# Seven products instead of eight for the second matrix of the block pairs too, with feature-major sums turned in 32x32 blocks and stored so

## The chip, the cores and the metric

The kernel runs on one core of one Trainium2 chip. The metric is the device time of one execution in microseconds (us); lower is better. The time before is the median of three runs, 1665.45 us (1663.57 to 1666.79).

## The reference

```python
# attention without softmax, per batch and head, then an RMS norm over the head's features
kv  = einsum('bhsd,bhse->bhde', k, v);  out = einsum('bhsd,bhde->bhse', q, kv)
x   = out / sqrt(mean(out*out, -1) + 1e-6) * g_norm      # as 4608 tokens x 512 features
# first layer:  w_in 512x2048, w_out 2048x512
x   = (s * max(x @ w_in1, 0)**2 + b) @ w_out1
# second layer, the same sizes
h   = x @ w_in2
out = (h * sigmoid(h)) @ w_out2                            # 4608 x 512, float32
```

## The kernel before, in words

The 4608 tokens are nine blocks of 512. Every factor of a product is split into a rounded part (hi) and a remainder (lo), and a product of 128x128 by 128x512 is three TensorE matmuls: hi by hi, hi by lo, lo by hi. Weights are decoded, split and, for the second layer, spilled to DRAM during the first layer (`decode`, `factors`, L234 to L356).

The first layer works block by block: a `unit` (16 per block) makes 128 hidden features (`mm1`, 12 matmuls) and adds their part to four output tiles (`mm2`, 12 matmuls).

In the second layer, blocks 0 to 7 go as four pairs, `tp` 0 to 3, and block 8 goes last, by units again. `pair_x` loads a pair and forms four differences of its quarters. `hidden(tp, j)`, for j 0 to 7 (`NS` = 8), makes 256 hidden features for the two blocks by Strassen's seven products instead of eight: 7 products x 2 halves x 3 = 42 matmuls at L839, into three PSUM banks X, Y, Z. VectorE adds the banks up at L864 (five instructions of a j), ScalarE copies one (L195), applies SiLU (L883, L885) and rounds the four results (`hi`, L188), and GpSimd or VectorE subtracts for the remainders (`lo`, L191).

`outputs(tp, j)` multiplies by the second matrix in the ordinary way, 8 token tiles (2 blocks x 4) x 2 halves f x 3 = 48 matmuls a j at L933, L934 and L935. The hidden tile is the stationary factor, and the weight tile moves, so a result is a tile of 128 tokens x 512 features in one of four PSUM banks `acc`. For j = 0 it is copied into one of eight tiles `y2`; for the others VectorE adds it to that tile (L943). After j = 7 each tile is stored by one DMA whose rows are 2 KB long (`store`).

All of it is ordered by `Plan`. Each piece of work is added with the engines that it may run on, a cost, a key (its due time), facts that it needs and makes, and the buffers that it takes and gives. `Plan.run` plays these costs through and emits the instructions in the order that results, each on one engine's in-order queue. All large DMAs are issued from SyncE's queue (SP) through the helper `dma` (L200). A wait therefore also holds all that is behind it on the same engine. Buffers: weight tiles of the first layer come free in its last block and are lent to the second layer (`wanted`, `lent_to`): 14 for the pair's split inputs `xo`, 6 for `win` (tiles of the first matrix), 5 for `wout` (of the second), 7 for `g2` (hi and lo of a hidden tile).

Of the kernel before, what the change touches and what calls it, by code (L numbers as in the profile page):

```python
# [15 lines left out]
class Plan:  # L16
# [12 lines left out]
    def __init__(self, room):  # L29
        self.room, self.ops, self.users, self.place = room, [], {}, {}  # L30
# [10 lines left out]
    def run(self):  # L41
# [6 lines left out]
        slots = {}  # L48
# [14 lines left out]
        def begin(e, op, when):  # L63
            t = max(free[e], when)
            for tag, _ in op[6]:
                s = slots.get(tag)
                if s is None:
                    room = self.room.get(tag, 1)
                    s = slots[tag] = [(0.0, i) for i in (range(room) if isinstance(room, int) else room)]
                if not s:  # L70
                    return None
                t = max(t, min(s)[0])
# [3 lines left out]
        while done < len(self.ops):  # L76
# [28 lines left out]
            for b in op[7]:  # L105
                users[b] -= 1
                known[b] = max(known.get(b, 0.0), end)
                if not users[b]:
                    slots.setdefault(b[0], []).append((known[b], self.place[b]))
# [10 lines left out]
def kernel(  # L120
# [40 lines left out]

    EXP_SCALE = 2.0 ** -112
# [36 lines left out]
    def dma(dst, src):  # L199
# [6 lines left out]
    plan = Plan({"g": 2, "acc": 4, "h": 2, "at": 2, "kv": 1, "rem": 1, "q": 1, "part": 2, "rms": 2, "gh": 3, "y": 2,  # L206
                 "raw": 4, "dw": 4, "raw2": 2, "dw2": 1, "tmp": 8})
# [367 lines left out]

    def place(b):

        tag = plan.place[b]
        return (pools["late"] if tag in [f"w{kd}{m}" for kd, m in late] else wp).tile([P, 2, DM], F32R, tag=tag, name=b[0])
# [17 lines left out]
    def unit(u):  # L597
# [7 lines left out]
        def w_gives(kind):  # L605
            if layer:
                return [("win" if kind == "i" else "wout", ("last", m))]
            return [(lent_to[f"w{kind}{m}"], f"w{kind}{m}")] if t == NB - 1 else []
# [9 lines left out]
        for kk in range(KD):  # L618
# [3 lines left out]
                gives=[xs_of(lb, kk)] * (m == KF - 1) + w_gives("i"))  # L622


        g = ("g", u)
        gs = ("gh", u)

        def first(e):
            g_t[u] = tp.tile([P, T], F32, tag="g", name="g", bufs=2)
# [13 lines left out]
        def pair():  # L643
            return (tp.tile([P, T], F32R, tag="gh", name="gh", bufs=3), tp.tile([P, T], F32R, tag="gl", name="gl", bufs=3))

# [11 lines left out]
        def g_hi(e):  # L657
            st["g"] = pair()
# [32 lines left out]
        for d in range(KD):  # L691
            acc = ("acc", (lb, d))
            add({"PE": 0.648}, u + LAG2 + d * 0.02, mm2(d),
                needs=[("gh", u), ("gl", u)] + ready("o") + [("mm2o", u - 1, d)] * (m > 0) + [("mm2o", u, d - 1)] * (d > 0),
# [15 lines left out]
    def block_out(layer, t, d, key, acc):  # L710
        lb = layer * NB + t
        st = {}
        yb = ("y", (lb, d))

        final = lb == 2 * NB - 1

        def out_y(e):
            if not final:
                st["y"] = tp.tile([P, T], F32, tag="y", name="y", bufs=2)
# [42 lines left out]
    def pair_x(tp, kk, key):  # L762
# [17 lines left out]
        def sub(o, a, b_, needs, takes=()):  # L780
# [4 lines left out]
            add(both(T), key + 1 + 0.1 * o, go, needs=needs, makes=[("pxs", o) + me], takes=takes)  # L785
# [308 lines left out]
```

## Time and profile before

| | |
|---|---|
| median of three runs | 1665.45 us |
| profiled execution, from first to last instruction (span) | 1664.5 us |
| TensorE busy | 98% of the span, 7762 matmuls |
| VectorE / ScalarE / GpSimd busy | 51% / 40% / 34% |
| DMA | 236.3 MB, 142 GB/s on average |
| granted TensorE clock | 0.999 of the full 2.4 GHz |

The profile shows one execution of the program. For each engine it gives the time in which the engine was busy; matmuls overlap one another in it, so the duration of one matmul (some 390 ns) is longer than the distance from one start to the next. Beside each wait it names what ended it. The profiled execution has no other time of its own than the span; it is 0.95 us less than the median of the runs.

In the trace, the first layer lasts to about 900 us, the pairs of the second layer from 902 us to about 1570 us (some units of block 8 are mixed in from 1559 us), and the units of block 8 from there to the end.

### The profile page before, as it was taken

How to read it: one execution, taken by the hardware profiler on the slowest of the kernel's cores; microseconds unless marked ns; L12 is line 12 of the kernel's file. 1: busy time of each engine (PE TensorE's matmuls, PEld its weight loads, DVE VectorE, ACT ScalarE, POOL GpSimd, SP SyncE). 2: the span in 40 equal slices, each digit the busy share in tenths (PEclk: the TensorE clock that was granted, in tenths of full speed). 3: DMA queues.
4: the chain of work that ended last, by engine and by line, in shares of the span. 5: the costliest groups of instructions: out<-in, count | busy, mean ns of one | idle time of the engine just before them, and what ended most of it. 6: DMA issues, size and time to landing. Idle time of an engine off the chain costs nothing.

```text
span 1664.5 us, 21283 instructions
## 1 busy us (share of the span) xinstructions
PE 1638.8 (98%) x7762; PEld 1331.6 (80%) x7762; DVE 846.4 (51%) x1301; ACT 664.5 (40%) x1205; POOL 569.6 (34%) x486
## 2 busy tenths in 40 slices
PE   8889999999999999999999999999999999999998
PEld 6667878888888888888887888888878888888887
DVE  5997555566655665534343244534453445244311
ACT  5776444444444444433333422432244224422322
POOL 3774343334434344210231222532253225222200
PEclk9999999999999999999999999999999999999999
DMA  9654335444444544310124444654455446544563
GB/s 217 175 161 137 124 122 158 126 163 134 138 139 129 168 119 155 104 68 0 51 79 145 124 142 141 198 181 140 141 191 181 140 141 203 179 141 140 184 190 108
DMA packets 227032, 236.30 MB, mean 142 GB/s; under 512 B 99952, under 2 KB 181872, under 8 KB 226800
## 3 DMA queue, kind: packets, MB, share of 16 engines
q1 hardware_dynamic: 226800, 234.94, 45.7%
q8 instruction: 62, 1.02, 0.3%
q14 instruction: 42, 0.34, 0.1%
q0 software_dynamic: 128, 0.00, 0.0%
HBM read 181.41 MB, written 53.48 MB: 141 GB/s over the span
## 4 chain that ended last, share of the span: by engine, by line
PE 90%; DVE 5%; issue 2%; DMA 1%; SPq 1%; ACT 1%; POOL 0%; DVEq 0%; POOLq 0%; ACTq 0%
PE hp L839 18%; PE h L184 8%; PE h L185 8%; PE h L183 8%; PE acc L183 8%; PE acc L184 7%; PE acc L185 7%; PE acc L934 7%; PE acc L935 7%; PE acc L933 7%; PE kv_ps L433 1%; DVE raw L263 1%; PE acc L686 1%; PE acc L687 1%; PE acc L688 1%
## 5 line engine op out<-in xcount | busy, mean ns | idle before, releaser
L839 PE MATMUL hp<-xo,win 128*128 128x512 f32 x1344 | 344.6, 391 | 1.8 <-DVE tmp L864 1.2
L191 POOL TENSOR_TENSOR g<-tmp,g 128x512 fp32r<-128x512 f32 x123 | 159.1, 1294 | 423.0 <-ACT g L188 215.5
L839 PEld LDWEIGHTS hp<-xo,win 128*128 128x128 f32 x1344 | 251.9, 188 | 59.4 <-DVE tmp L864 3.0
L943 DVE TENSOR_TENSOR y<-acc,y 128x512 f32<-128x512 f32 x224 | 154.2, 690 | 274.9 <-PE acc L935 272.7
L630 ACT ACTIVATE g<-h 128x512 f32<-128x512 f32 x160 | 95.3, 596 | 352.4 <-PE h L185 352.4
L183 PE MATMUL acc<-gh,wo 128*128 128x512 f32 x576 | 232.6, 404 | 0.0
L184 PE MATMUL acc<-gl,wo 128*128 128x512 f32 x576 | 225.7, 392 | 4.3 <-POOL gl L191 3.3
L185 PE MATMUL h<-xh,wi 128*128 128x512 f32 x576 | 225.6, 392 | 3.4 <-DVE wi L191 3.4
L184 PE MATMUL h<-xl,wi 128*128 128x512 f32 x576 | 226.0, 392 | 1.5 <-POOL xl L191 0.8
L183 PE MATMUL h<-xh,wi 128*128 128x512 f32 x576 | 226.4, 393 | 0.3 <-ACT g L630 0.3
L185 PE MATMUL acc<-gh,wo 128*128 128x512 f32 x576 | 225.4, 391 | 0.6 <-DVE wo L191 0.6
L935 PE MATMUL acc<-wout,g 128*128 128x512 f32 x512 | 201.7, 394 | 0.0
L934 PE MATMUL acc<-wout,g 128*128 128x512 f32 x512 | 201.6, 394 | 0.0
L638 DVE SCALAR_TENSOR_TENSOR g<-g,vecs 128x512 f32<-128x512 f32 x128 | 102.5, 801 | 194.3 <-ACT g L630 194.1
L933 PE MATMUL acc<-wout,g 128*128 128x512 f32 x512 | 201.2, 393 | 0.0
L864 DVE TENSOR_TENSOR tmp<-hp,tmp 128x512 f32<-128x512 f32 x160 | 110.3, 690 | 98.6 <-PE hp L839 93.2
L191 POOL TENSOR_TENSOR spill<-dw,spill 128x512 fp32r<-128x512 f32 x57 | 76.2, 1337 | 177.0 <-ACT spill L188 166.8
L666 DVE SCALAR_TENSOR_TENSOR gl<-g,vecs,gh 128x512 fp32r<-128x512 f32 x128 | 110.4, 863 | 47.3 <-ACT gh L660 46.3
L282 POOL TENSOR_TENSOR dw<-raw 128x256 uint32<-128x256 uint32 (+1 forms) x100 | 87.2, 872 | 137.8 <-DVE raw L268 70.4
L185 PEld LDWEIGHTS h<-xh,wi 128*128 128x128 f32 x576 | 108.5, 188 | 28.0 <-DVE wi L191 5.0
L184 PEld LDWEIGHTS h<-xl,wi 128*128 128x128 f32 x576 | 108.6, 188 | 25.8 <-POOL xl L191 1.4
L184 PEld LDWEIGHTS acc<-gl,wo 128*128 128x128 f32 x576 | 108.4, 188 | 25.4 <-POOL gl L191 4.2
(120 smaller groups left out, 2296.6 us busy)
## 6 DMA issues: line engine op xcount, KB each, us to landing
win<-wi SPq DMA_DIRECT2D x96, 512.0 KB, 4.3
wout<-wo SPq DMA_DIRECT2D x160, 256.0 KB, 4.2
wi<-spill SPq DMA_DIRECT2D x32, 512.0 KB, 2.6
wo<-spill SPq DMA_DIRECT2D x32, 512.0 KB, 2.7
win<-wi SPq DMA_DIRECT2D x64, 256.0 KB, 3.0
raw<-in_moe_w_out_dram SPq DMA_DIRECT2D x38, 256.0 KB, 3.2
y<-y SPq DMA_DIRECT2D x36, 256.0 KB, 2.8
raw<-in_moe_w_in_dram SPq DMA_DIRECT2D x34, 256.0 KB, 2.9
```

The source lines that it names most:

```text
L183: nc.tensor.matmul(ps, wh, xh, start=first, stop=False)
L184: nc.tensor.matmul(ps, wh, xl, start=False, stop=False)
L185: nc.tensor.matmul(ps, wl, xh, start=False, stop=last)
L191: eng[e].tensor_tensor(lo, src, f32(hi), op=ALU.subtract)
L638: nc.vector.scalar_tensor_tensor(out=g_t[u], in0=g_t[u], scalar=s_t, in1=g_t[u], op0=ALU.mult, op1=ALU.mult)
L666: nc.vector.scalar_tensor_tensor(out=st["g"][1], in0=g_t[u], scalar=b_t, in1=f32(st["g"][0]), op0=ALU.add, op1=ALU.subtract)
L839: nc.tensor.matmul(ps, w[:, wn, f_], x_[:, xn], start=first and n == 0, stop=kk == KH - 1 and n == 2, skip_group_check=True)
L864: nc.vector.tensor_tensor(t, bank[me, a], tmp[b_, me], op=ALU.add)
L933: nc.tensor.matmul(ps, g[:, 0, dd], w[:, 0], start=f == 0, stop=False)
L934: nc.tensor.matmul(ps, g[:, 0, dd], w[:, 1], start=False, stop=False)
L935: nc.tensor.matmul(ps, g[:, 1, dd], w[:, 0], start=False, stop=f == 1)
L943: nc.vector.tensor_tensor(y2[tp, tt], st["ps"], y2[tp, tt], op=ALU.add)
```

## The change

`outputs` is done by seven products as well. For each pair there are now four groups `q` of two `j` each, and for each q the seven products (`ORDER`) by two feature tiles (`KH` = 2): 14 steps of 2 x 3 matmuls, where two j had 16 steps of six. The weight tile is now the stationary factor, and a hidden tile moves, so the sums `y2` are 128 features x 512 tokens, fourteen of them for a pair (tiles `ya`). For this `hidden` forms, from its four SiLU results, four differences (`minus`) and splits seven tiles instead of four; the second matrix is loaded with all seven combinations (7 tiles of 512 KB for two j, was 4). At the end of a pair, `results` combines the 14 sums by 14 additions on GpSimd into eight tiles, VectorE turns each in 32x32 blocks (`turn_y`), and four DMAs store each tile in pieces of 32 features, 128 bytes.

The buffers change with it: `win` 5, `wout` 4, `g2` 8 lent tiles and two new ones, and the first layer's `gh` tiles join them (`heir`), thirteen in all; the 14 `ya` tiles are the first layer's `xh` and `xl` (eight), two `g`, two `y` and one lent weight tile in halves. `both2` gives the planner higher costs for two-input instructions.

```diff
+    def both2(n):
+        return {DVE: 0.15 + n * 2.05e-3, POOL: 0.15 + n * 2.25e-3}
...
@@ hidden
-        for f, n, src, ready, kk in ((0, 0, "d", ...), (1, 1, "b", ...), (1, 0, "c", ...), (0, 1, "a", ...)):
...
+        add(both2(T), kt, minus("e", "a", "d"), needs=sg("a", "d"), makes=sg("e"), takes=[tb["e"]])
+        add(both2(T), kt + 0.02, minus("f", "b", "e"), needs=sg("b", "e"), makes=sg("f"), takes=[tb["f"]])
+        add(both2(T), kt + 0.01, minus("a", "b", "a"), needs=sg("b", "e"), makes=sg("a2"))
+        add(both2(T), kt + 0.1, minus("c", "c", "f"), needs=sg("f") + [("gl",) + me + (B21,)], makes=sg("c2"))
+        for i, src, ready, kk, gives in (
+            (B11, "d", sg("d"), k(3) + 0.1, []), (B22, "b", sg("b"), k(4) + 0.2, []), (B21, "c", sg("c"), k(5) + 0.2, []),
+            (T1, "e", sg("e"), kt + 0.03, []), (T3, "a", sg("a2"), kt + 0.05, ["a"]), (T2, "f", sg("f"), kt + 0.07, []),
+            (T4, "c", sg("c2"), kt + 0.12, ["c"]),
+        ):
...
+            add(act(T), kk, hi, needs=ready, makes=[("gh",) + me + (i,)], takes=[gb])
+            add(both2(T), kk + 0.03, lo, needs=[("gh",) + me + (i,)], makes=[("gl",) + me + (i,)],
...
+    ORDER = (B11, B22, B21, T1, T3, T2, T4)
+    NG = NS // 2
...
@@ wout_loads: one tile for a product i of two j
+                for a in range(2):
+                    dma(f32(t)[:, a], w2_d["o", 2 * q + a][:, i])
...
@@ outputs
-                    for f in range(2):
-                        g, w = g2[me, f, n], wo_t[tp, j, f]
-                        nc.tensor.matmul(ps, g[:, 0, dd], w[:, 0], start=f == 0, stop=False)
-                        nc.tensor.matmul(ps, g[:, 0, dd], w[:, 1], start=False, stop=False)
-                        nc.tensor.matmul(ps, g[:, 1, dd], w[:, 0], start=False, stop=f == 1)
+        steps = [(i, d) for i in ORDER for d in range(KH)]
+        for n, (i, d) in enumerate(steps):
...
+                for a in range(2):
+                    (gh, gl), w = g2[(tp, 2 * q + a), i], wo_t[tp, q, i][:, a]
+                    nc.tensor.matmul(ps, w[:, 0, dd], gh, start=a == 0, stop=False)
+                    nc.tensor.matmul(ps, w[:, 0, dd], gl, start=False, stop=False)
+                    nc.tensor.matmul(ps, w[:, 1, dd], gh, start=False, stop=a == 1)
...
+                if q == 0:
+                    y2[tp, i, d] = sums(ya)
+                    copy(e, y2[tp, i, d], st["ps"])
+                else:
+                    nc.vector.tensor_tensor(y2[tp, i, d], st["ps"], y2[tp, i, d], op=ALU.add)
...
+    def results(tp):
+        key = base(tp) + 4 * NS + 8 + LAG3
+        for d in range(KH):
...
+            for n, (i, j, needs, gives) in enumerate((
+                (T2, B11, [t(T2), t(B11)], []), (B21, B11, [t(B21), t(B11)], [B11]), (T3, T2, [t(T3), o(0)], []),
+                (B22, T1, [t(B22), t(T1)], []), (B22, T2, [o(3), o(0), o(2)], [T2]), (T1, T3, [o(2), o(3)], []),
+                (T4, T3, [t(T4), o(2), o(5)], [T3]),
+            )):
...
+                add({POOL: 1.3}, key + 0.02 * n, go, needs=needs + ([o(0)] if n == 1 else []), makes=[o(n)], gives=[y(x) for x in gives])
+            for c, n, i, ready in ((0, 0, B21, 1), (0, 1, B22, 4), (1, 1, T1, 5), (1, 0, T4, 6)):
...
+                def turn_y(e, st=st, z=z, i=i, d=d):
+                    st["z"] = sums(z)
+                    nc.vector.transpose(st["z"], y2[tp, i, d])
...
+                    for a in range(P // Q):
+                        dma(out[r:r + T, f_ + a * Q:f_ + (a + 1) * Q].rearrange("(b r) d -> r b d", r=Q),
+                            st["z"][a * Q:(a + 1) * Q].rearrange("p (b d) -> p b d", d=Q))
+                add(dve(T), key + 0.2, turn_y, needs=[o(ready)], makes=[("yz", tp, c, n, d)], takes=[z], gives=[y(i)])
+                add({"SP": 1.92}, key + 0.3, store, needs=[("yz", tp, c, n, d)], makes=[("out", tp, c, n, d)], gives=[z], move=1.2)
...
@@ unit: block 8's second matrix starts only behind the last step of the pairs
+                + [("omo", NPR - 1, NS // 2 - 1, 13)] * (layer == 1 and m == 0),
...
-        wanted = [f"xo{i}{kk}" for i in range(7) for kk in range(KH)] + ["win"] * 6 + ["wout"] * 5 + ["g2"] * 7
+        wanted = [f"xo{i}{kk}" for i in range(7) for kk in range(KH)] + ["win"] * 5 + ["wout"] * 4 + ["g2"] * 8 + ["ya"]
```

How the change moves the work shows at three places. In the rows, a line's number is that of the kernel it stands in, the tile written is left of the arrow, and a wait stands in brackets (a name such as DMAHW3 is a DMA's semaphore). In the program of before, `y` is also the name of the tiles that hold `y2`.

TensorE, in the middle of the first pair: a step of `outputs` between products of `hidden` (`hp`), before.

```order
L933 MATMUL acc<-wout,g_8620 128x512
L934 MATMUL acc<-wout,g_8620 128x512
L935 MATMUL acc<-wout,g_8620 128x512
L839 MATMUL hp<-xo_7731,win 128x512 [waits DMAHW3_49,DVE_49]
L839 MATMUL hp<-xo_7731,win 128x512 x2
L839 MATMUL hp<-xo_7940,win 128x512 x3
L933 MATMUL acc<-wout,g_8566 128x512
```

The same place now.

```order
L993 MATMUL acc<-g_8559,wout 128x512 [waits DMAHW6_49]
L994 MATMUL acc<-g_8559,wout 128x512
L995 MATMUL acc<-g_8559,wout 128x512
L993 MATMUL acc<-g_8729,wout 128x512 [waits DMAHW7_49]
L994 MATMUL acc<-g_8729,wout 128x512 [waits Pool_49]
L995 MATMUL acc<-g_8729,wout 128x512
L875 MATMUL hp<-xo_7960,win 128x512 x3
```

A step is six matmuls as before, and its two halves now take the hidden tiles of two j as the moving factor. The pairs' steps are 224 now and were 256, and all that TensorE does ahead of the pairs is the same.

SyncE's queue, where the first pair's results are stored, before.

```order
L200 DMA wout<-wo_1_92 128x2x256 [waits DMAHW1_49]
L200 DMA out_dram<-y_8374 128x512 [waits DMAHW2_49,DVE_49]
L200 DMA out_dram<-y_8380 128x512 [waits DMAHW3_49,DVE_49]
L200 DMA out_dram<-y_8395 128x512 [waits DMAHW4_49,DVE_49]
L200 DMA out_dram<-y_8417 128x512 [waits DMAHW5_49,DVE_49]
L200 DMA out_dram<-y_8435 128x512 [waits DMAHW6_49,DVE_49]
L200 DMA x_9524<-y_81 128x2x512 [waits DVE_49,DMAHW7_49,Activation_49,Pool_49]
```

The same place now.

```order
L199 DMA win<-wi_2_85 128x1024 [waits DMAHW6_49,PE_49]
L199 DMA out_dram<-ya 32x16x32 [waits DMAHW7_49,DVE_49]
L199 DMA out_dram<-ya 32x16x32 [waits DMAHW0_49]
L199 DMA out_dram<-ya 32x16x32 [waits DMAHW1_49]
L199 DMA out_dram<-ya 32x16x32 [waits DMAHW2_49]
L199 DMA wout<-wo_0_91 128x512 [waits DMAHW3_49,PE_49]
L199 DMA wout<-wo_1_92 128x512 [waits DMAHW4_49]
L199 DMA win<-wi_2_85 128x512 [waits DMAHW5_49,PE_49]
```

Eight stores of a pair have become 32, each of 512 pieces, and they stand between loads of weights; they come behind the loads of the next pair's inputs, where five of eight stood ahead of the second of these.

ScalarE, where the next pair's first sums are copied out of PSUM, before.

```order
L195 COPY y_9655<-acc 128x512 [waits DMAHW2_49,PE_49]
L195 COPY y_9664<-acc 128x512 [waits DMAHW3_49,PE_49]
L195 COPY y_9669<-acc 128x512 [waits DMAHW4_49,PE_49]
L883 ACTIVATE tmp<-hp 128x512 [waits PE_49]
L188 ACTIVATE g_9685<-tmp 128x512 [waits Activation_49]
L195 COPY y_9691<-acc 128x512 [waits DMAHW5_49,PE_49]
```

The same place now.

```order
L194 COPY ya<-acc 128x512 [waits PE_49]
L919 ACTIVATE tmp<-hp 128x512 [waits PE_49]
L187 ACTIVATE g_9924<-tmp 128x512 [waits Pool_49]
L187 ACTIVATE g_9926<-tmp 128x512 [waits Activation_49]
L194 COPY ya<-acc 128x512 [waits DMAHW2_49,DMAHW6_49,DMAHW1_49,DMAHW7_49,DMAHW0_49,PE_49]
L194 COPY ya<-acc 128x512 [waits DVE_49,PE_49] x2
L921 ACTIVATE tmp<-tmp 128x512 [waits DVE_49]
```

A copy that took a tile waited for one store to land; now six of the fourteen copies wait for the four stores of a tile, and the others for the additions on GpSimd or the turns on VectorE. Behind them on ScalarE are the readings of the banks `hp` that TensorE fills next.

## Rows read from the trace of the kernel before

**Rows 1.** The profile page: span and busy time of each engine.

```profile
span 1664.5 us, 21283 instructions
PE 1638.8 (98%) x7762; PEld 1331.6 (80%) x7762; DVE 846.4 (51%) x1301; ACT 664.5 (40%) x1205; POOL 569.6 (34%) x486
```

**Rows 2.** Waits of TensorE from 900 to 1560 us: total, times, longest.

```profile
PE hp L839 <- DVE tmp L864: 1.2, 2, 0.8
PE hp L839 <- POOL xo L191: 0.6, 1, 0.6
```

**Rows 3.** Windows: length, busy of PE, PEld, DVE, ACT, POOL, clock, DMA share, GB/s.

```profile
920.00:1060.00 140.00, 140.00 (x612) 114.43 (x611) 55.87 (x81) 45.16 (x74) 41.64 (x33) 1.00 0.43 134
1060.00:1100.00 40.00, 40.00 (x174) 32.21 (x173) 21.59 (x29) 18.07 (x30) 21.35 (x16) 1.00 0.72 246
1100.00:1220.00 120.00, 120.00 (x524) 97.94 (x523) 49.27 (x72) 36.48 (x60) 35.35 (x28) 1.00 0.47 145
1390.00:1430.00 40.00, 40.00 (x176) 32.68 (x175) 19.95 (x28) 17.66 (x30) 18.81 (x14) 1.00 0.74 250
```

**Rows 4.** Timeline of TensorE in the first pair's stretch, start and duration in us.

```profile
1121.30 0.40 PE L933 MATMUL acc<-wout,g 128*128 128x512 f32 x1
...
1122.69 1.52 PE L839 MATMUL hp<-xo,win 128*128 128x512 f32 x6
1124.06 0.40 PE L933 MATMUL acc<-wout,g 128*128 128x512 f32 x1
```

**Rows 5.** Timeline, TensorE, two steps of the second pair's stretch, spaced more closely.

```profile
1222.04 0.39 PE L933 MATMUL acc<-wout,g 128*128 128x512 f32 x1
...
1223.39 1.52 PE L839 MATMUL hp<-xo,win 128*128 128x512 f32 x6
```

**Rows 6.** Groups by form, POOL and DVE, 920 to 1550 us: busy us, mean ns.

```profile
L191 POOL TENSOR_TENSOR g<-tmp,g 128x512 fp32r<-128x512 f32 x116 | 150.0, 1294 | 380.7 <-PE acc L935 194.9 <-ACT g L188 173.3 <-PE hp L839 6.2
L784 POOL TENSOR_TENSOR xt<-x,xt 128x512 f32<-128x512 f32 x10 | 15.7, 1566 | 4.5 <-DMA x<-y 4.0
L943 DVE TENSOR_TENSOR y<-acc,y 128x512 f32<-128x512 f32 x211 | 145.2, 690 | 263.4 <-PE acc L935 261.2 <-DMA win<-wi 2.1
L191 DVE TENSOR_TENSOR g<-tmp,g 128x512 fp32r<-128x512 f32 x5 | 7.7, 1530 | 3.6 <-ACT g L188 3.6
```

**Rows 7.** Groups by form, all of the span.

```profile
L191 DVE TENSOR_TENSOR gl<-g,gh 128x512 fp32r<-128x512 f32 x16 | 11.1, 692 | 74.4 <-ACT gh L188 74.4
L536 DVE STREAM_TRANSPOSE sq<-rms 128x512 f32<-128x512 f32 x36 | 25.5, 707 | 0.9
L885 ACT ACTIVATE tmp<-tmp 128x512 f32<-128x512 f32 x96 | 60.6, 632 | 158.2 <-DVE tmp L864 158.1
```

**Rows 8.** The profile page, DMA issues: count, KB each, median us to landing.

```profile
wout<-wo SPq DMA_DIRECT2D x160, 256.0 KB, 4.2
out_dram<-y SPq DMA_DIRECT2D x32, 256.0 KB, 6.0
q<-in_q_dram SPq DMA_DIRECT2D x112, 72.0 KB, 2.9
```

**Rows 9.** DMA view, 240 to 250 us: packets, and the queue's share of 16 engines.

```profile
DMA packets 253, 0.97 MB, mean 97 GB/s; under 512 B 16, under 2 KB 16, under 8 KB 253
q1 hardware_dynamic: 253, 0.97, 24.6%
```

**Rows 10.** The same view, 360 to 370 us.

```profile
DMA packets 3443, 1.82 MB, mean 182 GB/s; under 512 B 2706, under 2 KB 3218, under 8 KB 3442
q1 hardware_dynamic: 3442, 1.80, 61.3%
```

**Rows 11.** Issues on SP's queue, by tile: ns min/median/max, first and last start.

```profile
L200 SPq DMA_DIRECT2D lent_wo<-in_q_dram x16: 465/500/1507, 3.2 to 17.5; - x16
L200 SPq DMA_DIRECT2D out_dram<-y x32: 332/356/713, 1065.7 to 1658.8; - x32
L200 SPq DMA_DIRECT2D out_dram<-x x8: 472/569/597, 1650.4 to 1661.2; - x8
```

**Rows 12.** Timeline of the end: TensorE's last matmul, and SP's last issues.

```profile
1659.01 0.39 PE L688 MATMUL acc<-wout,gl 128*128 128x512 f32 x1
1659.37 2.40 SPq L200 DMA_DIRECT2D out_dram<-x  x4
```

More of the change, by code (lines that the diff above doesn't have):

```diff
@@ L47, in run @@
         ready = {e: {} for e in engines}
-        slots = {}
+        slots = {tag: [(0.0, i) for i in (range(n) if isinstance(n, int) else n)] for tag, n in self.room.items()}
         users = dict(self.users)
@@ L65, in begin @@
             for tag, _ in op[6]:
[L66 to L69, printed above, removed]
+                s = slots.setdefault(tag, [(0.0, 0)])
                 if not s:
@@ L160 @@
     NPR = (NB - 1) // 2
+    NTMP = 9
     EXP_SCALE = 2.0 ** -112
@@ L621, in unit @@
                 makes=[("mm1", u, kk)], opens=[("mm1o", u, kk)], takes=[("h", u)] * (kk == 0),
-                gives=[xs_of(lb, kk)] * (m == KF - 1) + w_gives("i"))
-        g = ("g", u)
-        gs = ("gh", u)
+                gives=([xs_of(lb, kk)] if lb != NB - 1 else [("ya", f"xh{kk}"), ("ya", f"xl{kk}")]) * (m == KF - 1) + w_gives("i"))
+        g = ("tmp" if layer else "g", u)
+        gs = ("g2" if layer else "gh", u)
+        if layer == 0 and u >= NB * KF - 3:
+            plan.heir[gs] = "g2"
+            if u >= NB * KF - 2:
+                plan.heir[g] = "ya"
         def first(e):
-            g_t[u] = tp.tile([P, T], F32, tag="g", name="g", bufs=2)
+            if layer:
+                g_t[u] = pools["l2p"].tile([P, T], F32, tag=f"tmp{plan.place[g]}", name="g")
+            else:
+                g_t[u] = tp.tile([P, T], F32, tag=plan.place[g], name="g")
             nc.scalar.activation(g_t[u], h_t[u], AF.Relu if layer == 0 else AF.Silu)
@@ new lines, in hidden, with minus, go @@
+            add(act(T), kk, silu, needs=ready, makes=[("sg", src) + me], takes=[tb["d"]] if src == "d" else [],
+                gives=[bk[X]] if src == "d" else [])
+        def minus(o, a, b_):
+            def go(e):
+                t = tmp[o, me] if (o, me) in tmp else new(o)
+                eng[e].tensor_tensor(t, tmp[a, me], tmp[b_, me], op=ALU.subtract)
+            return go
+        sg = lambda *names: [("sg", x) + me for x in names]
+        kt = k(6) + 0.2
+        add(both2(T), kt, minus("e", "a", "d"), needs=sg("a", "d"), makes=sg("e"), takes=[tb["e"]])
@@ L1054 @@
                 win_loads(pr, j)
+                hidden(pr, j)
+            for j in range(NG):
                 wout_loads(pr, j)
-                hidden(pr, j)
                 outputs(pr, j)
+            results(pr)
         load_x(2 * NB - 1, KF * (2 * NB - 2) + 2)
@@ L1062 @@
             unit(u)
+        for kk in range(KD):
+            for x in "hl":
+                plan.settle(("ya", f"x{x}{kk}"), f"x{x}{kk}")
         plan.run()
```

158 lines of the change are left out of this document (90 added, 68 removed).

## The prediction

> **What bounds the kernel now.** I read the page's busy times first, then TensorE's waits in the stretch that the change touches, then that stretch by windows, and last single rows for the prices. The page shows TensorE busy for 98% of 1664.5 us [rows 1]. The reader is to see next that between 900 and 1560 us it waited three times, 1.8 us in all [rows 2], and that VectorE, ScalarE and GpSimd are busy for some 30 to 55% of the windows there [rows 3]. So the pairs' stretch is bound by the number of matmuls, and work taken from TensorE there shortens the kernel until something else comes late. The cause for that would stand at the end of a pair, where DMA is already busy for 72 and 74% of a 40 us window, against 43 to 47% between [rows 3].
>
> **The price of a matmul.** The windows from 920 to 1060 and from 1100 to 1220 us hold 612 and 524 matmuls in 260 us with no gap [rows 3]: 0.229 us each. Six of `outputs` take 1.39 us from start to start, the six of `hidden` behind them 1.37 us [rows 4]; 0.231 is the price of a removed one. In some steps six take 1.35 us, 0.225 each [rows 5], so the rate depends on something that these rows don't name; I keep 0.225 and 0.234 (the two sides of the common 0.231) as bounds for the new form, whose stationary factor is the weight tile. The duration of a matmul is 0.39 us [rows 4], and by that the sum would be 75 us instead of 44. The Trainium skill, Perfetto Trace Analysis, Identifying the Most-Contended Engine, warns that matmul busy time tells little of the headroom, since matmuls are pipelined; the rows agree, as starts stand 0.23 us apart.
>
> **What is removed.** A pair had 8 j x 48 matmuls of `outputs`; now it has 4 q x 84. That is 48 less per pair and 192 in all, 1344 for 1536. 192 x 0.231 = **44.4 us** off the path. With all 1344 at 0.225 it would be 8 us more, at 0.234 4 us less. The 1344 matmuls of `hidden` and all of the first layer stay as they are.
>
> **What is added beside TensorE.** A pair lasts 672 x 0.229 = 154 us now, where it lasted 165.
>
> - GpSimd: by the order it gets some 82 two-input instructions a pair, of which 14 are the additions of `results`. At 1294 ns, the usual price, that is 106 us; at 1566 ns, the dearest row, 128 [rows 6].
> - VectorE: some 43 two-input instructions on SBUF, between 692 ns [rows 7] and 1530 ns [rows 6]; 82 evictions of PSUM at 690 ns [rows 6], fewer than before, since `outputs` has 14 for 16; and 8 turns, for which I take the 707 ns of the transposes of the same size [rows 7]. Together 92 to 128 us.
> - ScalarE: three more roundings a j at about the 632 ns of its other SBUF passes [rows 7], 15 us a pair on an engine that was busy for about a third.
>
> None of these reaches 154 us, so on average TensorE covers them. If that cover went, GpSimd would be the first to show, at 128 of 154.
>
> - Loads: the second matrix is 14.7 MB a pair instead of 8.4. The view from 240 to 250 us, with nearly no small packets, gives 24.6% of 10 us for 0.97 MB, 2.54 us of all sixteen engines for 1 MB [rows 9]. The added 6.3 MB take 16 us, spread over the pair.
> - Stores: a tile is 2048 pieces of 128 bytes. From 360 to 370 us, 61.3% of 10 us less 1.80 MB x 2.54 leaves 1.56 us for 2706 small packets, 0.58 us for a thousand [rows 10]. A tile then takes 0.67 + 1.19 = 1.85 us, the eight of a pair 14.8 us, where 2 KB rows took 5.3. These small packets are reads; for writes this is an estimate from them.
>
> In sum a pair has 25 us more of DMA: 49% of 165 us was 81 (43% of 140 and 72% of 40 us [rows 3]), now 107 of 154. In the 40 us at a pair's end it is 29 [rows 3] + 9.5 + 4 = 43 us: full, by little.
>
> - SP's queue: 32 issues of stores at a pair's end for eight. A similar load of 18 x 32 pieces takes 465 to 1507 ns to issue, median 500 [rows 11]; so 15 to 48 us. By the order the eight turns lie within 1.4 j of `hidden`, some 95 matmuls or 22 us. At the median the issues fit.
> - What is queued behind: loads of `win` and `wout` stand between the stores. A pair uses 32 `win` tiles, one in 4.8 us; with five tiles, four may be ahead, 19 us, less the landing, 4.2 us for the like loads [rows 8]: loads may come 15 us late before TensorE stands.
>
> **The waits at a pair's end** are the unknown. The 14 `ya` tiles hold a pair's sums until GpSimd has added, VectorE has turned and the stores have landed. On ScalarE six copies of the next pair's first sums wait for stores, on VectorE turns wait for GpSimd; the readings of `hidden`'s banks stand behind both, and TensorE waits for those. Before, copies also waited for a store's landing, 6.0 us at the median [rows 8], and the longest wait of TensorE was 0.8 us [rows 2]. So the lower bound is nothing; the upper, by 48 us of issues in 22, is 26 late less 15 of cover, 11 us a boundary. I take 2.5 us, near the lower bound, since median issues and transfers just fit, at three boundaries (the fourth lies beside block 8): **+7.5 us**.
>
> **Start and end.** In the first two j there are no steps of `outputs` between, and remainders lag: **+1 us** (the row before shows 0.8 [rows 2]). At the end, steps of `outputs` no longer stand between the last units, and the last four tiles of block 8 come together. SP then has eight issues of 0.57 us [rows 11] behind the first, where four took 2.40 us after the last matmul [rows 12]: 2.3 us more, of which 1.3 are won by the first tile's being done earlier. **+1 us.** A unit's SiLU, rounding and remainder, 0.6 + 0.6 + 0.7 us [rows 7], are covered by 12 matmuls, 2.7 us, so nothing more.
>
> **The sum:** 1664.5 - 44.4 + 7.5 + 1 + 1 = 1629.6, against the profiled execution's 1664.5 us, which has no time but its span and lies 0.95 us below the median of the runs: **1630 us**.
>
> **Rivals.**
>
> 1. *Clean boundaries and closely spaced steps.* If the stores hide as those of before did, and the new form runs at 0.225, the time is 1664.5 - 44.4 - 8 + 2 = 1614 us. For it: the waits of before. Against: most steps ran at 0.23.
> 2. *Short writes cost more than short reads.* At twice the price eight tiles take 29.6 us of DMA, the 40 us window holds 58, and loads come 18 us late, 3 more than the cover: 9 us at three boundaries, 1639. At two and a half times it is 25 late and 10 uncovered, 1661. I put this case at 1650. No row has many such writes. The Trainium skill, DMA: Bandwidth & Descriptors, Specifications, gives 512 bytes as the least for full rate and has smaller transfers done as read-modify-write; no run here shows it yet. By that rule the doubling, 1639 us, is the nearer end.
> 3. *The stores' landings become a chain* (the side of slower). If each tile's landing lets the next one go, a tile takes 4 issues of 0.5 us and a landing of 6.0 [rows 8, 11], 8 us, and eight take 64 where the order gives 22. Of the 42 us, four PSUM banks cover about 11 (four steps of 2.7 us with `hidden` between); 31 us are lost at three boundaries, 93 in all: 1664.5 - 44.4 + 2 + 93 = 1715 us. It decides from 14 us a boundary on. For it: six of fourteen copies wait for four landings each. Against: two to four tiles can be on their way at once, and the eight landings that were waited for cost nothing before.
>
> That the change doesn't remove the matmuls can be left out, as the order shows them gone.
>
> **How the numbers follow.** My forecast, 1620 to 1640, has 0.58; the first rival 0.16, the second 0.15, the third 0.11. What a measurement here can tell from no change is about 0.2%, 3.3 us: faster is below 1662. A fifth of the second rival, 0.03, falls within that of no change; so faster 0.86, same 0.03, slower 0.11. The range reaches from the first rival's 1614 to 1653, past the middle of the second, and leaves out the third and the second's dear end.
>
> **What would show it.** In the profile after, TensorE has 192 matmuls less and is still 97 to 98% busy; windows inside a pair show 0.225 to 0.234 us a matmul and no wait; the added wait stands in the 40 us after each pair's last step, ended by VectorE's readings of `hp` or ScalarE's copies, a few us each; the short stores land in 3 to 7 us and DMA is full there. It is wrong if waits stand inside the pairs (GpSimd or VectorE as the bound), if `win` or `wout` loads end TensorE's waits for long, or if the boundaries lose over 14 us.

## The result and the profile after

The changed kernel takes 1642.05 us (median of four runs, 1636.43 to 1645.23), beside 1664.51 us for the kernel before on the same chip: a ratio of 0.986, 95% interval 0.984 to 0.988. It is faster by 22 us; the forecast was 1630 us in a range of 1614 to 1653.

The page after, to be read beside [rows 1]:

```profile
span 1642.4 us, 21521 instructions
PE 1604.2 (98%) x7570; PEld 1298.9 (79%) x7570; DVE 1021.1 (62%) x1417; ACT 729.3 (44%) x1325; POOL 803.3 (49%) x626
```

TensorE has 192 matmuls less and is still 98% busy, so the page alone shows no loss. The waits do: the kernel after, TensorE from 900 to 1560 us, beside [rows 2].

```profile
PE hp L875 <- DVE tmp L900: 8.7, 7, 2.4
PE hp L875 <- DMA win<-wi: 2.9, 2, 1.8
PE acc L993 <- DMA wout<-wo: 1.0, 2, 0.6
PE acc L993 <- DVE ya L1002: 0.4, 1, 0.4
```

13.0 us of waits where there were 1.8. L900 is VectorE's reading of the banks of `hidden` (L864 before). The windows of the kernel after tell where they lie, with the columns of [rows 3]:

```profile
920.00:1060.00 140.00, 137.59 (x600) 111.99 (x599) 89.71 (x105) 70.16 (x118) 93.63 (x64) 1.00 0.63 195
1060.00:1100.00 40.00, 37.56 (x156) 30.17 (x156) 35.03 (x40) 16.38 (x28) 36.41 (x25) 0.96 0.70 205
1080.00:1090.00 10.00, 7.62 (x27) 5.83 (x26) 6.30 (x9) 4.16 (x7) 10.00 (x8) 0.85 0.59 156
1100.00:1220.00 120.00, 119.34 (x518) 96.58 (x517) 82.10 (x96) 57.25 (x97) 80.94 (x56) 1.00 0.73 213
1240.00:1250.00 10.00, 7.96 (x30) 6.13 (x29) 6.66 (x9) 4.16 (x7) 10.00 (x8) 0.87 0.62 168
```

Inside a pair (1100 to 1220 us) nearly nothing is lost. Around the first pair's last step (its last matmul of `outputs` starts at 1091.1 us), GpSimd is busy for 36.4 of 40 us and VectorE for 35.0, and for all of the two short windows GpSimd does not stop. One of these places step by step, from the timeline of the kernel after (engines in turn, start and duration in us, in brackets the idle time before and what ended it):

```profile
1078.02 3.45 POOL L1027 TENSOR_TENSOR ya<-ya 128x512 f32<-128x512 f32 x2
1081.43 1.28 POOL L929 TENSOR_TENSOR tmp<-tmp 128x512 f32<-128x512 f32 x1
...
1082.75 1.15 ACT L187 ACTIVATE g<-tmp 128x512 fp32r<-128x512 f32 x2 [3.48 <-POOL tmp L929]
...
1079.12 1.18 DVE L929 TENSOR_TENSOR tmp<-tmp 128x512 f32<-128x512 f32 x1
...
1083.41 2.79 DVE L190 TENSOR_TENSOR g<-tmp,g 128x512 fp32r<-128x512 f32 x2 [2.48 <-ACT g L187]
1086.13 0.68 DVE L900 TENSOR_TENSOR tmp<-hp,tmp 128x512 f32<-128x512 f32 x1
...
1086.86 2.92 PE L875 MATMUL hp<-xo,win 128*128 128x512 f32 x6 [2.38 <-DVE tmp L900]
1089.58 0.63 PE L993 MATMUL acc<-g,wout 128*128 128x512 f32 x1
```

Two additions of `results` on GpSimd (L1027) stand in front of a difference of the hidden tiles (`minus`, L929); ScalarE waits for that difference before it rounds; VectorE's remainders (L190) wait for the rounding, and the bank reading that TensorE needs is queued behind them. TensorE stands for 2.38 us. This is 4 us ahead of the pair's last step: the additions begin (1067.9 us) as soon as the sums that they need are complete, while the last steps still run. The six matmuls then take 2.72 us to the next start, where six took 1.37 [rows 4]: the granted clock of this window is 0.85, part of it at 1.2 instead of 2.4 GHz.

**Where the 22.1 us between the spans come from**, by starts on TensorE's timeline: from the first matmul of the pairs to the last of all, 757.0 us before (901.99 to 1659.01) and 729.8 after (905.80 to 1635.63), 27.2 less. Against 44.4 us of matmuls removed, 17.2 were given back. 2.0 of these are in the first two j (waits of 1.0 and 1.8 us where one of 0.8 stood); 15.2 are the rest and fall to the three pair ends: all other gaps of over 0.3 us between starts, but for 0.2 us, stand from 1039 to 1110, 1199 to 1290 and 1361 to 1442 us. Waits are 13.0 - 1.8 = 11.2 of the 17.2; the lower clock took some 2.8 more (10 us at 0.85 and 10 us at 0.87 in the short windows); the last 3 us are not assigned. The first layer ended 3.8 us later (905.80 against 901.99), and from the last matmul to the end of the span it is 6.8 us instead of 5.5. -27.2 + 3.8 + 1.3 = -22.1.

### The profile page after: what moved, and what is told of

Its sections match the earlier page's. It is cut to its first block, busy times and chain, and to the rows that moved or that the text cites. A ratio compares the mean times of both kernels' runs of the same rounds, so it can differ in the third digit from the quotient of the medians.

```text
span 1642.4 us, 21521 instructions
## 1 busy us (share of the span) xinstructions
PE 1604.2 (98%) x7570; PEld 1298.9 (79%) x7570; DVE 1021.1 (62%) x1417; ACT 729.3 (44%) x1325; POOL 803.3 (49%) x626
## 4 chain that ended last, share of the span: by engine, by line
PE 78%; DVE 7%; DMA 4%; POOL 4%; issue 3%; ACT 2%; SPq 1%; POOLq 0%; DVEq 0%; ACTq 0%
PE hp L875 14%; PE h L183 8%; PE h L184 8%; PE h L182 8%; PE acc L182 8%; PE acc L183 7%; PE acc L184 7%; PE acc L993 5%; PE acc L995 4%; PE acc L994 4%; SPq L199 1%; PE kv_ps L436 1%; DVE g L190 1%; DMA x<-y 1%; POOL xo L190 1%
## 5 line engine op out<-in xcount | busy, mean ns | idle before, releaser
L875 PE MATMUL hp<-xo,win 128*128 128x512 f32 x1344 | 341.1, 395 | 11.6 <-DVE tmp L900 8.7
L190 POOL TENSOR_TENSOR g<-tmp,g 128x512 fp32r<-128x512 f32 x132 | 188.8, 1436 | 168.7 <-ACT g L187 165.4
L182 PE MATMUL acc<-gh,wo 128*128 128x512 f32 x576 | 233.3, 405 | 0.0
L183 PE MATMUL acc<-gh,wo 128*128 128x512 f32 x576 | 226.3, 393 | 4.8 <-POOL gh L190 3.4
L184 PE MATMUL acc<-gh,wo 128*128 128x512 f32 x576 | 225.7, 392 | 0.0
L993 PE MATMUL acc<-g,wout 128*128 128x512 f32 x448 | 177.1, 395 | 1.6 <-DMA wout<-wo 1.0
L995 PE MATMUL acc<-g,wout 128*128 128x512 f32 x448 | 175.5, 392 | 0.0
L994 PE MATMUL acc<-g,wout 128*128 128x512 f32 x448 | 175.3, 391 | 0.0
L187 ACT ACTIVATE g<-tmp 128x512 fp32r<-128x512 f32 x224 | 138.5, 631 | 77.1 <-POOL tmp L929 44.9
L190 POOL TENSOR_TENSOR spill<-dw,spill 128x512 fp32r<-128x512 f32 x57 | 77.4, 1358 | 176.5 <-ACT spill L187 171.1
L1002 DVE TENSOR_TENSOR ya<-acc,ya 128x512 f32<-128x512 f32 x168 | 113.4, 683 | 76.4 <-PE acc L995 72.8
L900 DVE TENSOR_TENSOR tmp<-hp,tmp 128x512 f32<-128x512 f32 x160 | 109.6, 685 | 71.5 <-PE hp L875 69.8
L190 DVE TENSOR_TENSOR g<-tmp,g 128x512 fp32r<-128x512 f32 x92 | 133.4, 1473 | 14.5 <-ACT g L187 13.4
L699 DVE SCALAR_TENSOR_TENSOR gh<-g,vecs,gh 128x512 fp32r<-128x512 f32 x128 | 110.8, 865 | 48.0 <-ACT gh L693 47.2
L184 PEld LDWEIGHTS h<-xh,wi 128*128 128x128 f32 x576 | 108.7, 189 | 29.9 <-DVE wi L190 7.2
```

Of the source, the lines that this page charges most:

```text
L182: nc.tensor.matmul(ps, wh, xh, start=first, stop=False)
L183: nc.tensor.matmul(ps, wh, xl, start=False, stop=False)
L184: nc.tensor.matmul(ps, wl, xh, start=False, stop=last)
L187: nc.scalar.activation(hi, src, AF.Copy)
L190: eng[e].tensor_tensor(lo, src, f32(hi), op=ALU.subtract)
L699: nc.vector.scalar_tensor_tensor(out=st["g"][1], in0=g_t[u], scalar=b_t, in1=f32(st["g"][0]), op0=ALU.add, op1=ALU.subtract)
```

## The experiments

Theory 1: GpSimd's additions of `results` and its dearer instructions hold the differences of the hidden tiles, and VectorE's queue passes that on to TensorE. Theory 2: the short stores fill the DMA engines and SyncE's queue, so weights come late. The table has all runs: median, stretch of the pairs and block 8 (from the first matmul of the pairs to the last of all), and TensorE's waits from 900 us to the end, by what ended them. Stretch and waits are of one profiled execution each, and the four executions of the changed kernel lay between 1636.43 and 1645.23 us; so a few us of stretch count only where the medians agree.

| kernel | median us | stretch | bank readings L900 (L864 before) | win, wout | others |
|---|---|---|---|---|---|
| before | 1664.5 | 757.0 | 1.2 | 0 | 0.6 |
| after | 1642.1 | 729.8 | 8.7 | 3.9 | 0.4 |
| again | 1642.8 | 730.1 | 8.4 | 4.1 | 0.2 |
| long_rows | 1638.6 | 728.0 | 11.5 | 1.2 | 0 |
| no_sums | 1634.6 | 723.8 | 3.0 | 5.1 | 0.2 |
| no_sums_long | 1627.5 | 716.2 | 3.1 | 1.4 | 0.7 |
| sums_both | 1650.9 | 737.8 | 5.7 | 6.4 | 4.5 |
| real_costs | 1641.9 | 731.6 | 4.5 | 2.1 | 10.1 |
| real_costs_lag2 | 1643.4 | 733.5 | 1.1 | 9.4 | 6.2 |
| act_queue_lag2 | 1691.2 | 782.4 | 18.5 | 0 | 29.9 |
| act_queue_costs | 1700.0 | 789.9 | 30.5 | 0 | 29.6 |
| split | 1641.7 | 728.0 | 9.2 | 3.3 | 0 |
| split_costs | 1644.0 | 732.4 | 4.6 | 3.0 | 10.2 |
| split_lag2 | **1629.7** | 717.8 | 1.1 | 0.4 | 5.5 |

### again: the changed kernel without an edit

> The changed kernel once more, without an edit. Theory 1 (GpSimd's additions at a pair's end hold the differences of the hidden tiles, and behind them VectorE's readings of the banks): the same stalls at the same three places, 15 to 19 us in all over the pairs, since the order of the queues fixes them. Theory 2 (the short stores hold up the loads of weights): the stalls lie where DMAs happen to collide, so they move between executions, and the waits for win and wout (2.9 and 1.0 us in the profile) come out otherwise by 2 us or more. Theory 3 (the 3.8 us by which the first layer ended later are chance of an execution): the first matmul of the pairs stands at 901 to 904 us, not at 905.8; if it is a consequence of the change, it stands at 905.8 again within 0.7.

The stalls stood at the same places with nearly the same lengths (1086.32, 1246.30, 1289.67 us; 730.1 - 712.6 = 17.5 us given back in all), so they come from the order and not from chance collisions. The pairs began at 905.32 us, which by the text speaks for a consequence of the change. But with the edits at the pairs' ends that follow, which leave the first layer as it is, they began at 904.5, 903.5, 900.9 and 902.0 us. So 3.8 us are within what this start varies by between such kernels; what makes it vary stays open.

### long_rows: stores with rows of 2 KB

```diff
-    for a in range(P // Q):
-        dma(out[r:r + T, f_ + a * Q:f_ + (a + 1) * Q].rearrange("(b r) d -> r b d", r=Q), ...)
+    r += (2 * c + d) * P
+    for a in range(P // Q):
+        dma(out[r + a * Q:r + (a + 1) * Q, :], st["z"][a * Q:(a + 1) * Q])
```

> The four stores of a result tile write 32 rows of 2 KB each in place of 512 pieces of 128 bytes, to another place of the output (so the output's tiles stand wrongly); number of stores, bytes, and the order on every engine stay. Theory 1: the stalls of TensorE behind VectorE's readings stay (8.7 us of waits), only waits for win and wout of 1 to 4 us go: 0 to 4 us faster than the changed kernel. Theory 2: 8 to 14 us faster, the boundaries' stalls fall from 17.4 to under 8 us.

3.4 us below the changed kernel's median, 4.2 below that of the run beside it. The waits that were left, of the kernel with long rows:

```profile
PE hp L875 <- DVE tmp L900: 11.5, 8, 2.7
PE acc L993 <- DMA wout<-wo: 1.2, 3, 0.5
```

No wait for `win` is left, but those for the bank readings rose by 3 us: what had waited for a load now waited for VectorE. With long rows a store's issue is shorter too (0.42 us at the median, 0.50 with short ones), so the run does not part the DMA engines' share from that of SyncE's queue. The short pieces are a real, smaller part, as theory 1 had it.

### no_sums: without the additions of results

```diff
 def go(e, d=d, i=i, j=j):
-    eng[e].tensor_tensor(y2[tp, i, d], y2[tp, i, d], y2[tp, j, d], op=ALU.add)
+    pass
```

> The 14 additions of results at each pair's end are left out on GpSimd (56 instructions in all, so the output is not the sum that it should be); everything else keeps its order, turns and stores among them. Theory 1: GpSimd is free for the differences of the hidden tiles, TensorE's waits for VectorE's bank readings at the three pair ends fall from about 7.7 to under 2.5 us, and with them the matmuls at half clock behind them: 7 to 12 us faster than the changed kernel. Theory 2: turns and stores start earlier but are as many, so no more than 3 us.

8.2 us faster than the changed kernel beside it. The waits for bank readings that are left, 3.0 us, are the two of the first two j; at the pair ends there is none. Theory 1 is shown for this part: the order on VectorE, ScalarE, TensorE and SyncE is the same in both kernels, and only the additions are gone. Two things go with them, though, their place in GpSimd's queue and their hold on VectorE: its remainders are as many in both kernels and shorter without the additions (kernel without additions, 920 to 1550 us; with them 92 took 1473 ns each, row further below). Which of the two is worth more is not told apart.

```profile
L190 DVE TENSOR_TENSOR g<-tmp,g 128x512 fp32r<-128x512 f32 x92 | 122.1, 1348 | 13.4 <-ACT g L187 11.7
```

In exchange TensorE waits for `win` a little longer (kernel without additions):

```profile
PE hp L875 <- DMA win<-wi: 4.3, 2, 3.5
PE hp L875 <- DVE tmp L900: 3.0, 2, 1.8
```

### no_sums_long: both taken out

The edit is the two above together.

> Both parts taken out together: the 14 additions of results of each pair are left out, and the stores write rows of 2 KB to another place (so the output is not the sum, and stands wrongly). Without the additions alone the kernel took 1634.6 us and TensorE still waited 4.3 us for win; with long rows alone it took 1638.6 and waited for no win at all. If the two losses are separate, they add: 4 to 6 us faster than without the additions, 1628.5 to 1630.5 us, with no wait for win over 0.5 us. If the wait for win comes from the load of the queues as a whole and not from the short pieces, 1633 to 1635 us.

1627.5 us, a little under the range for adding losses. With the work gone, the two losses add (15.3 us below the run of the changed kernel, where the two alone gave 8.2 and 4.2): the stretch is 716.2 us, against 757.0 - 44.4 = 712.6 for the matmuls removed and nothing given back, and most of the 3.6 us between are the waits in the first two j.

### sums_both: the additions on either engine

```diff
-add({POOL: 1.3}, key + 0.02 * n, go, ...)
+add(both2(T), key + 0.02 * n, go, ...)
```

> The 14 additions of results may go on VectorE or GpSimd, whichever the planner finds free, at the planner's cost of a two-input instruction on either. Theory 1: the load at a pair's end is only shared out; VectorE is itself over 90 per cent busy there, and its additions stand in front of its bank readings, so -6 to +4 us against the changed kernel, with fewer waits only if the differences come 3 us or more earlier. Theory 2: within 2 us of the changed kernel, since the stores are the same.

8 us slower, outside both ranges. At the first pair's end the last addition starts sooner (1098.8 us instead of 1108.5), but the first tile is turned later (1098.2 instead of 1080.2), and 20 of the 32 stores come in one row, in front of the loads (SyncE's queue of this kernel, start and length):

```profile
1111.02 12.72 SPq L199 DMA_DIRECT2D out_dram<-ya  x20
1123.83 0.93 SPq L199 DMA_DIRECT2D wout<-wo  x2
1124.86 1.32 SPq L199 DMA_DIRECT2D win<-wi  x3
```

TensorE waits 2.9 us at 1129.78 for this `win`. VectorE does not help either: it was itself busy for 28.1 of the 30 us from 1080 on. How much of the 8 us each of the two took is open.

### real_costs and real_costs_lag2: the planner's prices, and a later second matrix

```diff
-    return {DVE: 0.15 + n * 2.05e-3, POOL: 0.15 + n * 2.25e-3}
+    return {DVE: 0.15 + n * 2.6e-3, POOL: 0.15 + n * 2.7e-3}
...
-    add({POOL: 1.3}, key + 0.02 * n, go, ...)
+    add({POOL: 1.55}, key + 0.02 * n, go, ...)
```

For real_costs_lag2 also `LAG3 = 2.0` for 0.6.

> Only the planner's prices change, to those that the trace shows: two-input instructions of 512 columns 1.48 us on VectorE (was 1.20) and 1.53 on GpSimd (was 1.30), the additions of results 1.55 (was 1.3). Same work, another order. If the stalls come from an order planned with too low prices (the bank readings of VectorE stand behind subtractions that take longer than planned), TensorE's waits for these readings fall from 8.4 to under 4 us and the time by 4 to 9 us, to 1634 to 1639 us. If GpSimd and VectorE simply have more to do at a pair's end than there is time for, the order cannot help: the waits move elsewhere, 1640 to 1646 us.

> The prices as in the kernel with the measured prices, and the second matrix's steps due later behind the hidden tiles that they use (2.0 in place of 0.6 units of the planner's time), which leaves the differences and remainders of the hidden tiles more room. If order and slack are what lacks, 2 to 5 us faster than with the prices alone, 1631 to 1637 us; if the load itself is the limit, within 2 us of it; if weights and hidden tiles are now held longer, so that their loads come later, waits for win or wout of over 3 us in all and 1642 to 1648 us.

Neither was faster than the changed kernel; both fell into the ranges in which waits move elsewhere. The prices did what they should (bank readings 8.7 to 4.5, with the lag 1.1 us), and the time went into other waits. With the prices alone TensorE waits three times, 2.7 to 2.8 us, for VectorE's evictions (L1002), in front of which VectorE had taken subtractions of the next pair's inputs; here its timeline in that kernel:

```profile
1053.58 0.68 DVE L929 TENSOR_TENSOR tmp<-tmp 128x512 f32<-128x512 f32 x1
1054.18 1.78 DVE L820 TENSOR_TENSOR x<-x 128x512 f32<-128x512 f32 x1
1055.89 1.76 DVE L820 TENSOR_TENSOR xt<-x,xt 128x512 f32<-128x512 f32 x1
1057.57 0.68 DVE L1002 TENSOR_TENSOR ya<-acc,ya 128x512 f32<-128x512 f32 x1
```

With the lag it waits 9.4 us for `win`, twice over 4.5.

### act_queue_lag2 and act_queue_costs: the stores from ScalarE's queue

```diff
-    dma(out[r:r + T, ...], st["z"][...])
+    nc.scalar.dma_start(out=out[r:r + T, ...], in_=st["z"][...])
...
-add({"SP": 1.92}, key + 0.3, store, ...)
+add({ACT: 0.24}, key + 0.3, store, ...)
```

> As the kernel with measured prices and the later second matrix (lag 2), but the 32 stores of a pair are issued from ScalarE's queue and no longer stand between the loads of weights on SyncE's queue. In the kernel that it is made from TensorE waits 9.4 us for win, twice 4.6 us behind the stores of a pair. If the loads are late because they stand behind the stores in SyncE's queue (a store there takes 0.34 to 2.1 us to issue), these waits fall under 3 us and the time by 5 to 9 us, to 1634 to 1638 us. If they are late because the DMA engines themselves are full of short pieces, the waits stay at 7 to 11 us and the time at 1641 to 1645 us. If the issue of a store takes ScalarE 0.5 us or more, its SiLU and roundings come late in turn: waits for VectorE's readings rise by over 4 us, 1644 us or more.

> The same move of the stores to ScalarE's queue on the kernel with measured prices and the lag as it was (0.6). There TensorE waits 2.1 us for win and 8.2 us for VectorE's additions to the sums (three times 2.7 us, ahead of the stores). The second wait has nothing to do with the stores and stays at 7 to 9 us; if SyncE's queue is what holds the loads, the first falls under 0.7 us: 1 to 3 us faster than that kernel, 1639 to 1641 us. If ScalarE suffers from the issues, 1643 us or more.

The waits for `win` went to nothing. In act_queue_lag2 SyncE issues four loads of `win` from 1103.35 us on; with the stores in its queue it had issued two from 1106.75 us and the next four only from 1123.53 us (rows further below). So it is the stores in SyncE's queue that hold the loads. But ScalarE pays far more than the 0.24 us a tile that the planner had: 48 and 58 us slower than the kernels they are made from. ScalarE, and below it TensorE, in the first of the two:

```profile
1103.22 6.57 ACTq L1040 DMA_DIRECT2D out_dram<-ya  x8
1109.89 0.59 ACT L194 COPY ya<-acc 128x512 f32<-128x512 f32 x1 [7.13 <-DMA out_dram<-ya]
...
1121.39 0.79 PE L993 MATMUL acc<-g,wout 128*128 128x512 f32 x1 [4.12 <-ACT ya L194]
```

Eight stores held ScalarE's queue for 6.57 us: four issues of 2.25 us from 1103.22, four of 2.29 us from 1107.51, and between them 2.0 us in which the queue stood until the first of these stores had landed (1107.43 us). The copy of the next pair's sum started only behind them, and TensorE stood for 1.4 us at 1111.54 for the copy of a bank that came next. At 1121.39 us, behind more stores on ScalarE, it waited 4.1 us for a copy of a sum. Both texts had this case, one with "1644 us or more", the other with "1643 us or more", and undersized it.

### split, split_costs, split_lag2: each store by itself, at its measured price

```diff
-    add({"SP": 1.92}, key + 0.3, store, ..., gives=[z], move=1.2)
+    for a in range(P // Q):
+        add({"SP": 0.55}, key + 0.3, store(a), ..., gives=[z], move=0.46)
```

`store(a)` issues the one store a of the four. The edit stands on the changed kernel (split), on real_costs (split_costs) and on real_costs_lag2 (split_lag2).

> As the kernel with measured prices and lag 2, stores on SyncE's queue, but the planner is told what a store takes there (0.55 us of the queue and 0.46 us of the DMA engines each, 2.2 and 1.84 a tile; it had 1.92 and 1.2) and may place each of the four by itself. If the planner only lacked the prices, loads of win move ahead of stores and the waits for win fall from 9.4 to under 5 us: 1637 to 1641 us. If the bytes in short pieces simply fill the stretch, it stays within 2 us of 1643 us.

> Only the stores of the changed kernel are edited as in the last run of the split stores: each of the four by itself and at 0.55 us of SyncE's queue and 0.46 us of the DMA engines for the planner; prices of the engines and the lag stay as in the changed kernel. If the two losses are separate, only the waits for win and wout go (4.1 us with what follows at half clock), and those for VectorE's bank readings stay at 7 to 11 us: 1636.5 to 1640 us, as with the long rows (1638.6). If the order of the stores was the whole of it and the other edits add nothing: 1628 to 1632 us. If the split alone does nothing: 1641 to 1645 us.

> The split stores on the kernel with measured prices of the engines, lag 0.6 as before. That kernel waited 8.2 us for VectorE's additions to the sums and 2.1 us for win. If the lag is what takes away the first wait (with lag 2.0 it was 3.1 us), it stays at 6 us or more here and the time at 1635 to 1641 us; if the stores' place alone brings it down, 1628 to 1632 us.

split_lag2 takes **1629.7 us** and leaves nothing out: ratio to the kernel before 0.979, 95% interval 0.978 to 0.981, and 12.4 us below the changed kernel's median. It was better than its text allowed. The same edit without the prices and the lag (split) or without the lag (split_costs) gave 1641.7 and 1644.0 us, no gain that shows; for split that was the last of its text's three cases, not the separate losses that were expected, and its stretch of 728.0 us is that of its fastest execution, 1638.56 us. split_costs kept its 8.2 us of waits for evictions, as one case of its text said, so it is the lag that takes those away; its time lies above that text's 1641 us. TensorE's waits in split_lag2:

```profile
PE acc L994 <- DVE g L190: 2.0, 1, 2.0
PE acc L993 <- DVE ya L1002: 1.9, 3, 0.7
PE hp L875 <- POOL xo L190: 1.6, 3, 0.6
PE hp L875 <- DVE tmp L900: 1.1, 1, 1.1
PE hp L875 <- DMA win<-wi: 0.4, 1, 0.4
```

SyncE's queue at the first pair's end, of real_costs_lag2:

```profile
1106.75 0.93 SPq L199 DMA_DIRECT2D win<-wi  x2
1107.77 8.12 SPq L199 DMA_DIRECT2D out_dram<-ya  x12
1115.99 2.08 SPq L199 DMA_DIRECT2D wout<-wo  x2
1118.17 4.29 SPq L199 DMA_DIRECT2D out_dram<-ya  x8
1122.56 0.92 SPq L199 DMA_DIRECT2D wout<-wo  x2
1123.53 2.08 SPq L199 DMA_DIRECT2D win<-wi  x4
```

and of split_lag2:

```profile
1105.90 2.59 SPq L199 DMA_DIRECT2D win<-wi  x3
1108.59 7.55 SPq L199 DMA_DIRECT2D out_dram<-ya  x9
```

The stores are as many and as short; one load more of `win` goes ahead of them, and the wait of 4.6 us behind them is 0.4. What follows: the loss at the pair ends was one of order, and not of too much work. No single repair of prices, lag or stores helped: each left the wait or moved it to the next resource that had no slack: GpSimd, VectorE's queue, or SyncE's. Whether the later second matrix with the split, but without the engines' prices, or the lag alone, would do as well was not tried.

## Why the prediction was right, and where it was off

The direction and the main term were right, and so was the kind of loss: waits around the pairs' ends, ended by VectorE's readings of `hp`. The number owes something to a wide range. 1642 us lies 12 us above the forecast and outside 1620 to 1640, which had the chance of 0.58; of the times named, the second rival's 1639 is the nearest, and its mechanism, dear writes, did not come.

- **The matmuls removed** (-44.4 us): right. 192 are gone, and inside a pair the price is about the old one, 0.230 us (119.34 us busy for 518 in the window from 1100 us); the first rival's 0.225 did not come, and its 1614 us with it.
- **The waits at a pair's end** (+7.5 us): what ends the waits was right, and the place nearly, but 15.2 us were lost, 5.1 a boundary. The step that failed is "None of these reaches 154 us, so on average TensorE covers them". It is true over a pair (from 1060 to 1220 us GpSimd and VectorE are busy for 117 us each of 160) and wrong for its end, where GpSimd has the 14 additions and the next pair's inputs at once; the 2.5 us were then weighed from stores and loads alone. no_sums gives 8.2 us of the 15.2 to GpSimd's additions, long_rows 3.4 to 4.2 to the short stores. TensorE's lower clock behind two of the waits had no term at all. The two longest waits for VectorE (2.38 and 2.04 us, at 1086.86 and 1246.88) stand 4 and 6 us ahead of their pairs' last steps, not behind them, since the additions begin before the last sums are done; so one sign of being wrong, waits inside a pair with GpSimd as the bound, came in small, in a pair's last 7 us. The sign of 14 us is, by the third rival, meant for each boundary.
- **The prices on GpSimd and VectorE**: the sum was bounded by 1294 and 1566 ns on GpSimd, and 692 to 1530 on VectorE [rows 6, 7]. After, by groups from 920 to 1550 us, columns as there:

```profile
L190 POOL TENSOR_TENSOR g<-tmp,g 128x512 fp32r<-128x512 f32 x132 | 188.8, 1436 | 168.7 <-ACT g L187 165.4 <-PE acc L995 2.6 <-DMA win<-wi 0.8
L929 POOL TENSOR_TENSOR tmp<-tmp 128x512 f32<-128x512 f32 x76 | 119.0, 1573 | 21.9 <-ACT tmp L921 13.7 <-DVE tmp L929 6.8
L1027 POOL TENSOR_TENSOR ya<-ya 128x512 f32<-128x512 f32 x44 | 66.0, 1522 | 13.0 <-DVE ya L1002 12.9
L190 DVE TENSOR_TENSOR g<-tmp,g 128x512 fp32r<-128x512 f32 x92 | 133.4, 1473 | 14.5 <-ACT g L187 13.4
L1002 DVE TENSOR_TENSOR ya<-acc,ya 128x512 f32<-128x512 f32 x164 | 110.8, 683 | 74.3 <-PE acc L995 70.8 <-DMA wout<-wo 3.4
L929 DVE TENSOR_TENSOR tmp<-tmp 128x512 f32<-128x512 f32 x52 | 60.6, 1164 | 19.7 <-POOL tmp L929 10.4 <-ACT tmp L921 8.6
```

  With both inputs in SBUF they lie in the middle between the bounds (L190 on GpSimd, L929 on VectorE), near the dear end or above it; evictions (L1002, one input in PSUM) took 683 ns. The planner had 1.30 and 1.20 us. The Trainium skill, SBUF — State Buffer, Who interferes with whom, states that a VectorE instruction with two SBUF inputs contends with a GpSimd instruction that reads SBUF, and that the port pair they share is an exclusive lock. The rows agree that the two slow each other: in the timeline above GpSimd's L929 takes 1.28 us while VectorE is idle, and its two L1027 before it, beside VectorE's L929, take 3.45.
- **The DMA terms**: right over a pair, 105 to 114 us of all engines where 107 were estimated. At a pair's end 43 of 40 us were estimated, and the fullest 40 us there were 0.85 to 0.91 busy. From 1275 to 1283 us of the kernel after, nearly all packets are of stores:

```profile
DMA packets 7355, 1.33 MB, mean 167 GB/s; under 512 B 7135, under 2 KB 7135, under 8 KB 7355
q1 hardware_dynamic: 7355, 1.33, 87.7%
```

  7.02 us of all engines, less 0.42 MB of other bytes at 2.54 us (1.06), is 0.83 us for a thousand pieces and 1.71 us a tile, where 1.85 was estimated from reads. The second rival (twice that) falls. The Trainium skill, DMA: Bandwidth & Descriptors, Specifications, gives 512 bytes as the least for full rate; the trace agrees that pieces under it are slow, 1.71 us a tile against 0.67 for its bytes at the rate of [rows 9], but shows no more for writes than for reads.
- **SyncE's queue**: the estimate of 15 to 48 us, median 16, was right in size, but the cover of 15 us was not all there: from 1274.5 us on 16 stores in one row took 8.8 us, and TensorE waited 1.8 us for the `win` behind them. The view of the store tile `out_dram` after (ns, lowest, median and highest issue; then us to landing):

```profile
L199 SPq DMA_DIRECT2D out_dram<-ya x128: 337/502/2093, 1081.0 to 1586.9; - x128
DMA to landing us min/median/max: 1.9/3.1/5.5
```

  Stores landed in 3.1 us, not the 6.0 that was feared, and no wait of TensorE here is ended by ScalarE's copies: the third rival, a chain of landings, did not form.
- **Start and end**: +2.0 and +1.3 us for +1 and +1. The first layer's 3.8 us had no term.

So the span missed the sum by 1642.4 - 1629.6 = 12.8 us: 7.7 at the pair ends, 3.8 in the first layer, 1.3 at start and end. That split_lag2 then took the forecast's 1630 us is partly chance: its stretch gave back 717.8 - 712.6 = 5.2 us where the sum had 8.5, and its pairs began 1.6 us later than those of before, for which the sum had nothing.

## What to carry to other kernels

A load that fits on average must be counted again for the stretch in which it comes together, engine by engine: here 128 of 154 us was fine, and 36 of 40 at a pair's end was not. When a hand-made or planned order fails at such a stretch, take the work out (additions, row length) to see what each part is worth, and then correct all the planner's prices at once, since a single correction only shows the next wait. Put no DMA issue on an engine whose compute others wait for unless its issue time, and the landings that it waits for, are counted as that engine's work.

## What was not expected

- Short stores hold the engine that issues them, by their issue and by waits for landings in the same queue: 8 stores took 6.57 us of ScalarE's queue, 4.5 of it issues (0.5 us each at the median, as on SyncE's) and 2.0 a landing. With all stores there the kernel was 48 us slower.
- A VectorE instruction with two SBUF inputs of 512 columns takes 0.68 to 1.78 us, by what GpSimd does at the time: in the timeline of real_costs above, L929 at 1053.58 began in a pause of GpSimd's (up to 1053.74 us), and L820 at 1054.18 while one of GpSimd's own ran (1053.74 to 1055.42).
- Behind a wait of 2.4 us TensorE ran six matmuls in 2.72 us, at a granted clock of 0.85 in that window: here the wait cost half as much again as it lasted. It need not: in real_costs the clock fell behind the wait of 2.71 us for L1002 at 1219.09 (0.83 from 1215 to 1225 us) and not behind that of 2.67 us at 1380.53 (1.00 from 1378 to 1388 us).
